# Another written-out order of 679 operations in an S4 convolution and MLP block

## The chip, the cores and the metric

The kernel runs on one core of a Trainium2 chip. The metric is the device time of one execution in microseconds. Five engines work side by side, each through its own queue in program order: TensorE (PE, matrix products; its weight loads are listed as PEld), VectorE (DVE), ScalarE (ACT), GpSimd (POOL) and SyncE (SP). DMA transfers are issued from the queues of SP and POOL.

## What is computed

```python
x = A_u                                   # 1 x 2048 x 512, bf16
h = x + A_ref(layernorm(x))               # S4 convolution
h2 = h + B_ref(layernorm(h))              # MLP
# A_ref: dt = exp(log_dt); K = Re sum_n C_n * exp(dt*A_n*l) * dt*B_n   (128 states n, 2048 lags l)
#        y = irfft(rfft(pad(u)) * rfft(pad(K)))[:2048] + u * Dskip
# B_ref: gelu(y @ w1 + b1) @ w2 + b2      (512 -> 1376 -> 512)
```

## The kernel before

**Two parts.** The front computes the convolution and its residual as 679 recorded operations; the MLP follows as plain code (`mlp`, L1179 and on) and isn't part of the order. The front works on all 2048 rows. Its channels come in two halves of 256 (0 and 1); only the normalisation and the first transform do both at once.

**How the order is set.** Each piece of work is recorded with `S.op` in class `Sched` (L133): the engine, or two allowed engines; what it must follow; which rotating buffer it takes (`acq`) and which it gives back (`rel`). `S.run(ORDER)` (L157 to L178) then emits them in the sequence of the list ORDER (L34). A step of the list is 2 × the operation's number, plus 1 where the second of the two allowed engines is taken; numbers below (#141) are those of operations. Only the relative order on one engine's queue matters for what is issued when; waits between engines follow from the data and the buffers. Two more things follow from the list: a rotating buffer is handed out at the step that takes it (three PSUM buffers "p" of 1024 f32 per partition, through which nearly all TensorE results of the front pass; five "s" for sines, four "a", two "u", two "kf", three "z"), and ScalarE's table set is switched where an operation needs the other set than the one before (L160: natural log and exponential, or sine).

**The stages**, with the lines of their instructions:

- Parameters (`params`, L494 and on): products of A, B, C and dt, exp(dt) (#32), polar form and phase pieces, which are turned by DMA transposes into PL, QL and TL.
- Tables (`tables`): phases by products of one-row operands (L393), sines of them (L126), the scaled half of the table M (L72 on VectorE or L95 on ScalarE; #136 and #141), sums that multiply bases with rows Dp spread by POOL DMAs (L469; L78), the sine of nn (L427, #150), the last rows of M put by SP (L482).
- The block matrix BD for the first transform (#6, L78).
- Normalisation (`norm_in`): sums and squares of six row groups on ScalarE (L876, L878), statistics of the other ten on VectorE (L880), the roots (#209), then 16 times: u (L891 on VectorE or L889 on ScalarE), two products aps (L896), eviction to `a` (L88 ScalarE, L90 VectorE), a DMA to A_dram (L905). When all 16 are written, four DMAs load X back in another layout (L917).
- The kernel of half 0: exponentials (L716), phase products pv and qv (L736, L771), their sines (L126), products Pt and Q (L78), then four groups of 128 small matmuls kps (L801; #334 to #343), evicted as ku, near and far (L805, L120), put to DRAM and read back as kt (L830 to L838).
- The kernel of half 1 in the same way: exponentials by scale (L685, L692, the product with amp at L696), sines, kps (#470, #473, #476, #479), kt (#482 to #488).
- Per half eight times: the spectrum kfps of the kernel (22 matmuls, L991 and L993), evicted to kf; the transform xps of X (8 matmuls, L934 to L937), evicted to X; their product pa (L78); the way back zps (L1026 to L1029), evicted to z, written to Zd (L1070) and turned by a DMA to ZT (L1064; for half 1 #590 to #640).
- Late in the front: W is cleared and filled (L961, L964), the first rows of half 0 (L1084, #659 and #662), and the first four rows of half 1 in four steps (#675 L1119 and L1121, #676 L1126, #677 and #678 L1131), between which stand the last two half ways back (#666, #668).
- The biases of the MLP (#492, L1152 to L1159) on POOL.

Many lines are those of small helpers: L72 and L74 (`ts`), L78 (`tt`), L88 and L90 (`evac`), L95 (`scaled`), L120 (`stt`), L126 (`sines`).

The emitting loop, which the change doesn't touch:

```python
for step in order:
    opts, fn, _, tag, rel = self.ops[step >> 1][:5]
    if tag:
        self.now[tag] = took[step >> 1] = ... room[tag].pop(0)
    fun = self.ops[step >> 1][7]
    if fun not in (None, held):
        held = fun
        self.sets(SETS[fun])
    fn(opts[step & 1][0]) if len(opts) > 1 else fn()
```

Of the kernel before, what the change touches and what calls it, by code (L numbers as in the profile page):

```python
# [31 lines left out]
AT = {"log": 1, "m0": 3, "m1": 3, "bases": 3, "sin0": 3, "exp": (1, 1), "sin": (3, 3)}  # L32
SETS = {1: "natural_log_exp_and_others", 3: "trig_and_small"}
ORDER = [  # L34
# [21 lines left out]
]  # L56


# [1416 lines left out]
```

## Time and profile before

| | |
|---|---|
| median of 3 runs | 271.67 us (270.72 to 272.27) |
| the profiled execution | 271.67 us |
| its span, first to last instruction | 269.9 us |
| PE busy | 235.5 us (87%) |
| DVE busy | 203.8 us (76%) |
| ACT busy | 177.8 us (66%) |
| POOL busy | 44.9 us (17%) |
| table loads on ACT | 7, 9.0 us |

The profile comes from one execution on the chip; all its times run from the start of the span. A row of the timeline gives the start, the duration, the engine, the line, the operation, the tile written and the tiles read, their shape, and in brackets how long the engine had been idle and what ended the idle time. A row of a group gives the busy time of all its instructions, the mean of one in ns, and the idle time ahead of them. A row of windows gives a stretch, its length, then for PE, PEld, DVE, ACT and POOL the busy time and the number of instructions, then the granted clock of TensorE as a share of full speed, the DMA engines' share and GB/s. A row of DMA issues ends with the median time from issue to landing.

### The profile page before, as it was taken

Reading aid. Unit: us, or ns where it says so; the run is one execution under the profiler, and the core shown is the slowest. Engines: PE = TensorE matmul, PEld = TensorE weight load, DVE = VectorE, ACT = ScalarE, POOL = GpSimd, SP = SyncE. Lnnn points to the kernel's source line nnn. Section 1 sums busy time; section 2 is a strip of 40 time slices with the busy share of each in tenths; the row PEclk is TensorE's granted clock in tenths of the full one; section 3 lists DMA queues with packets and bytes.
Section 4 is the critical chain, followed back from the end, with each engine's and each line's share of the span. In section 5 each row is a group of like instructions: output and inputs, shape, how many; then the busy total and the mean of one; then the engine's idle time right before and its main releaser. Section 6 shows DMA issues by size and latency. Waiting matters only on the chain.

```text
span 269.9 us, 6075 instructions
## 1 busy us (share of the span) xinstructions
PE 235.5 (87%) x2369; PEld 152.3 (56%) x2386; DVE 203.8 (76%) x450; ACT 177.8 (66%) x281; POOL 44.9 (17%) x108
## 2 busy tenths in 40 slices
PE   2749966668972999999999999999999999999995
PEld 2413322225740576879988888887864544544443
DVE  3879999999989889999487675889973773772022
ACT  5599999998999988986255255645850730731720
POOL 8752069300001300010033420010000000000000
PEclk9855569999965599999999999999999999999999
DMA  5800266959778559513049499697914014013101
GB/s 137 297 15 1 40 120 137 214 136 179 79 150 256 170 164 350 160 39 87 10 114 251 120 254 261 181 265 217 268 29 107 23 31 105 19 27 94 39 19 58
DMA packets 54968, 35.24 MB, mean 131 GB/s; under 512 B 29050, under 2 KB 53132, under 8 KB 54684
## 3 DMA queue, kind: packets, MB, share of 16 engines
q1 hardware_dynamic: 53036, 30.05, 42.8%
q0 software_dynamic: 1904, 4.81, 7.3%
q8 instruction: 18, 0.29, 0.5%
q14 instruction: 10, 0.08, 0.1%
HBM read 18.65 MB, written 11.21 MB: 111 GB/s over the span
## 4 chain that ended last, share of the span: by engine, by line
PE 64%; DVE 20%; ACT 7%; issue 3%; DMA 3%; SPq 1%; DVEq 0%; ACTq 0%
PE kfps L993 13%; PE o2ps L1279 13%; PE h1ps L1267 13%; PE kps L801 5%; DVE Pt L78 3%; DMA x<-in_A_u_dram 3%; DVE M L78 3%; PE y L1084 2%; DVE a L90 2%; DVE st L880 2%; PE qv L771 2%; PE kfps L991 2%; DVE u L891 2%; PE xps L934 1%; ACT u L876 1%
## 5 line engine op out<-in xcount | busy, mean ns | idle before, releaser
L1269 ACT ACTIVATE hT<-h1ps,b_sb 128x512 bf16<-128x512 f32 (+3 forms) x55 | 32.0, 612 | 36.7 <-PE h1ps L1267 36.7
L993 PE MATMUL kfps<-kt,M 128*128 128x256 bf16 x320 | 40.5, 277 | 0.0
L1267 PE MATMUL h1ps<-y2T,w 128*128 128x512 bf16 (+3 forms) x217 | 39.9, 336 | 0.6 <-DVE y2T L90 0.5
L1279 PE MATMUL o2ps<-w_sb,hT 128*128 128x512 bf16 (+3 forms) x183 | 38.5, 366 | 0.2
L993 PEld LDWEIGHTS <-M 128*128 128x128 bf16 x320 | 31.9, 100 | 4.9 <-issue 0.5
L78 DVE TENSOR_TENSOR ot<-o2ps,h 128x512 bf16<-128x512 f32 (+1 forms) x17 | 11.1, 659 | 30.8 <-PE o2ps L1279 19.0
L1267 PEld LDWEIGHTS <-w 128*128 128x128 bf16 (+1 forms) x220 | 21.9, 100 | 15.2 <-issue 0.6
L1279 PEld LDWEIGHTS <-hT 128*128 128x128 bf16 (+1 forms) x187 | 18.2, 98 | 19.7
L88 ACT CAST kf<-kfps 128x1024 bf16<-128x1024 f32 (+1 forms) x14 | 13.3, 953 | 11.1 <-PE kfps L993 9.3
L126 ACT ACTIVATE sq<-qv 128x1024 bf16<-128x1024 int16 x20 | 19.9, 1049 | 1.1 <-PE qv L771 0.5
L78 DVE TENSOR_TENSOR Pt<-s,Pt 128x1024 bf16<-128x1024 bf16 x32 | 20.2, 687 | 0.0
L801 PEld LDWEIGHTS <-Pt 128*32 128x32 bf16 x1024 | 17.9, 169 | 3.4 <-DVE far L120 1.5
L801 PE MATMUL kps<-Q,Pt 128*32 128x20 bf16 x1024 | 18.7, 221 | 0.6 <-DVE far L120 0.5
L896 PE MATMUL aps<-u,BD 128*128 128x512 bf16 x29 | 10.5, 455 | 10.0 <-DVE u L891 6.7
L78 DVE TENSOR_TENSOR pa<-X,kf 128x1024 bf16<-128x1024 bf16 (+1 forms) x17 | 11.2, 658 | 7.1 <-ACT kf L88 6.7
L126 ACT ACTIVATE s<-pv 128x1024 bf16<-128x1024 int16 x16 | 16.1, 1047 | 0.3 <-DVE Pt L78 0.3
L469 POOL DMA_DIRECT2D Dp<-Dd x24 | 13.4, 566 | 14.6 <-DVE M L78 14.6
L88 ACT CAST z<-zps 128x1024 bf16<-128x1024 f32 x10 | 10.2, 1020 | 7.6 <-PE zps L1029 5.4
L90 DVE CAST a<-aps 128x1024 bf16<-128x1024 f32 x11 | 13.3, 1219 | 0.0
L78 DVE TENSOR_TENSOR Q<-sq,Q 128x1024 bf16<-128x1024 bf16 x20 | 13.2, 688 | 0.0
L771 PE MATMUL qv<-RQ,QL 128*128 128x128 bf16 (+1 forms) x60 | 10.9, 293 | 2.4 <-ACT sq L126 1.1
L78 DVE TENSOR_TENSOR pa<-pa,pb 128x512 bf16<-128x512 bf16 (+1 forms) x34 | 12.4, 407 | 0.6
(245 smaller groups left out, 476.0 us busy)
## 6 DMA issues: line engine op xcount, KB each, us to landing
A_dram<-a SPq DMA_DIRECT2D x16, 256.0 KB, 2.6
X<-A_dram SPq DMA_DIRECT2D x4, 1024.0 KB, 8.2
Zd<-z SPq DMA_DIRECT2D x14, 256.0 KB, 3.2
ZT<-Zd SPq DMA_DIRECT2D x12, 256.0 KB, 3.6
x<-in_A_u_dram SPq DMA_DIRECT2D x4, 512.0 KB, 8.5
out_dram<-ot SPq DMA_DIRECT2D x15, 128.0 KB, 1.7
w_sb<-in_B_w_dram SPq DMA_DIRECT2D x1, 1280.0 KB, 6.8
Dp<-Dd POOLq DMA_DIRECT2D x8, 128.0 KB, 3.5
```

Source lines behind the costliest of these rows:

```text
L78: nc.vector.tensor_tensor(out, a, b, op)
L88: nc.scalar.copy(out, in_)
L90: nc.vector.tensor_copy(out, in_)
L126: nc.scalar.activation(out, v.bitcast(i16)[..., 0:2 * n:2], ACT.Sin, scale=S2PI / 65536)
L469: nc.gpsimd.dma_start(t[o::128 // cnt], bass.AP(row.tensor, row.offset + 1024 * kh, [[0, cnt], [1, 1024]]))
L771: nc.tensor.matmul(v[:, n], lhsT=K.QL[(b + n) // 8][:, (b + n) % 8, :], rhs=K.RQ[:, m0:m1].rearrange("p i c d -> p (i c d)"), start=True, ...
L801: nc.tensor.matmul(kps[32 * g:32 * g + 32, i // 8, at:at + 20], lhsT=Pt[:, :, u, c], rhs=Q[:, :, u, c], start=True, stop=True, tile_positi ...
L896: nc.tensor.matmul(ps[:, h, :], lhsT=K.BD[:, h].rearrange("p a b -> p (a b)"), rhs=cell["u"][:], start=True, stop=True)
L993: nc.tensor.matmul(ps[:, k, c, :], lhsT=K.M[:, t, 2 * k2 + k, c, :], rhs=kt[:, t, :], start=(c == 1 and t == 0), stop=(t == 4))
L1267: nc.tensor.matmul(pt[:fs, 0:n], lhsT=K.w1_sb[:, dc, fc * P:fc * P + fs], rhs=y2T[tb][:, dc, js, :].rearrange("p a b -> p (a b)"), start=( ...
L1269: nc.scalar.activation(hT[tb % 2][:fs, fc, cols], pt[:fs, 0:n], ACT.Gelu_apprx_tanh, bias=K.b1_sb[:fs, fc:fc + 1], scale=1.0)
L1279: nc.tensor.matmul(pt[:], lhsT=h[:fs, fc, jj * P:(jj + 1) * P], rhs=K.w2_sb[:fs, fc, d], start=(fc == 0), stop=(fc == NFC - 1))
```

## The change

Only the list ORDER is another one; it holds the same 679 numbers, a few of them with the other engine. The list is long, so its first, a middle and its last lines stand here:

```diff
 ORDER = [
-    36, 38, 40, 42, 44, 46, 54, 56, 58, 60, 82, 0, 2, 78, 62, 66, 86, 68, 370, 984, 366, 8, 74, 76, 362, 80, 10, 12, 4, 364, 84, 296, 64, 198, 6, 88, 70, 128, 92, 298, 130,
-    132, 374, 378, 376, 72, 380, 94, 274, 372, 382, 134, 384, 136, 160, 90, 164, 138, 368, 392, 284, 48, 140, 124, 142, 390, 96, 166, 388, 278, 144, 126, 146, 396, 168, 148,
...
-    874, 1036, 1038, 862, 924, 876, 864, 726, 1040, 1130, 946, 992, 928, 728, 666, 948, 994, 746, 866, 930, 996, 934, 950, 27, 730, 926, 878, 998, 872, 748, 1046, 25, 936,
...
-    1270, 1272, 773, 1274, 776, 1276, 1286, 1152, 1288, 1085, 1302, 1290, 1306, 1258, 1310, 1318, 1154, 1218, 1324, 1292, 1312, 1278, 1294, 1296, 1320, 1304, 1308, 1314,
-    1326, 1260, 1316, 1330, 1332, 1338, 1341, 1328, 1334, 1350, 1220, 1280, 1344, 1298, 1336, 1352, 1354, 1343, 1346, 1300, 1348, 1356, 1322
+    74, 76, 370, 54, 60, 58, 82, 66, 0, 78, 296, 70, 80, 2, 62, 8, 362, 4, 84, 86, 88, 56, 64, 364, 10, 366, 68, 128, 198, 298, 6, 300, 130, 378, 264, 368, 72, 90, 132, 376,
+    372, 160, 380, 292, 134, 374, 406, 136, 266, 294, 92, 94, 382, 138, 96, 46, 164, 384, 278, 140, 48, 124, 268, 44, 142, 166, 98, 396, 144, 148, 102, 146, 390, 388, 168,
...
+    910, 726, 912, 866, 1036, 944, 714, 874, 728, 860, 926, 920, 914, 946, 876, 746, 878, 716, 948, 950, 742, 990, 1038, 952, 20, 745, 1040, 1126, 954, 748, 958, 992, 956,
...
+    1270, 1218, 772, 777, 1284, 1272, 1274, 1302, 1286, 1180, 1276, 1288, 1324, 1258, 1306, 1318, 1220, 1290, 1292, 1320, 1326, 1278, 1294, 1296, 1241, 1310, 1312, 1200,
+    1304, 1330, 1308, 1261, 1314, 1328, 1280, 1344, 1298, 1316, 1334, 1322, 1350, 1332, 1352, 1338, 1340, 1336, 1343, 1346, 1300, 1348, 1354, 1356
 ]
```

What this does to each engine's queue, by a comparison of the two orders instruction by instruction:

- **ScalarE.** exp(dt) (#32) comes ahead of the sine of BD's factors (#5), the table set changes there once more: eight table loads (L160) for seven. The sine of nn (#150) moves from behind the polar steps to the third place of the queue, ahead of all sums of x. The scale of M (#141) goes to VectorE. Of the u, three (#242, #226, #266) for two (#238, #250) are on ScalarE; of the evictions `a` ahead of the second exponentials it takes five, as before, but others (#216, #228, #244, #268 and #240 for #264, #236, #212, #232 and #240). In half 0's sines the first six are of p, then those of q. In half 1, eleven sines (three p, eight q) stand in a row behind the second exponentials, ahead of the first eviction of a spectrum (#534); before, four stood there.
- **VectorE.** It takes #141 and one u fewer; BD (#6) moves from the third place of the queue to just ahead of spread_p (#55), near the last statistics; two products with amp (#407, #413) stand ahead of the last `a` (#272) where one (#413) stood ahead of the last `a` (#256). It evicts seven spectra kf ahead of the end where it evicted three, and two z instead of four. At the end the first early rows (#660, #663) stand ahead of product #656, the statistics (#661) ahead of the last z (#671).
- **TensorE.** The same operations stand ahead of the first spectrum, which is #513 instead of #503. Ahead of the first kernel product of half 1 (#470) stand, beside what stood there before, spectra #533 and #523, phase products #461, #464, #467 and #431; spectrum #563, phase product #455 and X products #357 and #371 now come behind it. Ahead of the last of the four (#479), spectrum #533 comes in, and X products #365 and #383 and ways back #498 and #568 go behind. At the end #675 stands ahead of #666.
- **POOL.** The biases (#492) go from the start of its queue to behind the clearing of W (#574) and the turn #522. Turns #552, #562, #620 and #630 go by POOL; #512, #502 and #542 go by SP. The put of far for half 0 (#347), the put of near for half 1 (#482) and the kt get #484 go by POOL; the put of far for half 1 (#483) and the kt get #486 by SP. Both residual loads (#579, #580), one load of W1 (#491) and all four fills of W go by SP.
- **SP.** The puts of `a` and the turns come in another sequence; the four X loads still stand behind all 16 puts.

32 rows, old and new, of the table ORDER are left out of this document.

## The prediction

> **What bounds the kernel now.** I read the windows first, cut where the stages change (columns: from:to, length, busy time of each engine with its instructions, granted TensorE clock, DMA share, GB/s).
>
> ```profile
> 20.00:90.00 70.00, 51.50 (x652) 23.74 (x657) 67.63 (x145) 68.52 (x111) 17.54 (x29) 0.77 0.62 128
> 90.00:105.00 15.00, 13.90 (x96) 9.73 (x97) 13.10 (x18) 14.06 (x27) 0.72 (x2) 0.89 0.73 229
> 105.00:183.00 78.00, 77.62 (x1122) 67.97 (x1124) 62.61 (x113) 45.63 (x52) 11.77 (x14) 1.00 0.59 164
> ```
> From 20 to 90 us VectorE (67.63) and ScalarE (68.52) fill the 70 us to 97 and 98%, and TensorE waits for them. From 105 to 183 us TensorE is busy 77.62 of 78 at full clock: 0.38 us is all the air there is. After that the MLP runs, which ORDER doesn't hold. So an order of the same operations can gain in three places: both elementwise engines reach the first spectrum sooner, the 15 − 13.90 = 1.10 us that TensorE idles from 90 to 105 closes, or the last rows come earlier. The chain of waits, second, agrees: TensorE holds 64% of it, VectorE 20%, ScalarE 7%.
>
> ```profile
> PE 64%; DVE 20%; ACT 7%; issue 3%; DMA 3%; SPq 1%; DVEq 0%; ACTq 0%
> ```
> Third, the timeline where one stage passes into the next (start, length, engine, line), and finer windows around it.
>
> ```profile
> 85.27 1.89 PE L896 MATMUL aps<-u,BD 128*128 128x512 bf16 x4 [4.92 <-DVE u L891]
> 90.89 2.34 PE L993 MATMUL kfps<-kt,M 128*128 128x256 bf16 x10
> 91.47 1.22 DVE L90 CAST a<-aps 128x1024 bf16<-128x1024 f32 x1
> 94.52 1.25 PE L993 MATMUL kfps<-kt,M 128*128 128x256 bf16 x10
> 96.50 5.78 SPq L917 DMA_DIRECT2D X<-A_dram  x4
> 102.38 0.28 PE L934 MATMUL xps<-X,M 128*128 128x256 bf16 x1 [0.24 <-ACT kf L88]
> ```
> ```profile
> 80.00:90.00 10.00, 4.29 (x11) 1.08 (x12) 10.00 (x16) 10.00 (x34) 2.42 (x4) 0.50 0.73 201
> 90.00:100.00 10.00, 9.47 (x63) 6.84 (x63) 8.52 (x12) 9.52 (x22) 0.72 (x2) 0.83 0.56 168
> 100.00:110.00 10.00, 9.38 (x76) 6.87 (x76) 9.54 (x16) 8.64 (x10) 0.00 (x0) 1.00 1.08 350
> ```
> TensorE waits 4.92 us for a VectorE `u`, its clock falls to 0.50, and the first half spectrum costs 2.34 instead of 1.25. The last eviction `a` ends at 91.47 + 1.22 = 92.69; the four X loads go out at 96.50 and the first product on X starts at 102.38.
>
> **The change part by part.** The comparison of the two orders shows the same operations, some on the other of their two allowed engines. The profiled execution took 271.67 us, the median of the three too (its span is 269.9, with 1.77 around it), so the sum is made on 271.67.
>
> *ScalarE up to the second set of exponentials.*
>
> ```profile
> L160 ACT ACT_TABLE_LOAD x7 | 9.0, 1283 | 0.9 <-PEq L1459 0.7
> 95.14 1.28 ACT L160 ACT_TABLE_LOAD   x1
> 96.44 2.03 ACT L126 ACTIVATE s<-pv 128x1024 bf16<-128x1024 int16 x2
> L95 ACT ACTIVATE M<-M,cols 128x2048 bf16<-128x2048 bf16 x1 | 2.0, 2019 | 0.0
> L889 ACT ACTIVATE u<-x,mv,r1y 128x512 bf16<-128x512 bf16 x2 | 1.7, 854 | 0.0
> L427 ACT ACTIVATE nn<-nn,pi_t x1: 847/847/847, 27.9 to 27.9; 128x672 f32<-128x672 int32 x1
> L876 ACT ACTIVATE u<-x 128x512 bf16<-128x512 bf16 x6 | 3.8, 631 | 2.3 <-DMA x<-in_A_u_dram 2.2
> ```
> The new order does exp(dt) (#32) ahead of the early sines, so the table set is switched once more: eight loads for seven. A load is 1283 ns and the next sine starts 96.44 − 95.14 = 1.30 later: +1.30. The scale of M (#141, L95) leaves for VectorE: −2.02. A third `u` comes: +0.85. The sine of nn (#150, 0.85) moves from 27.9 us into the 2.2 us in which ScalarE waits for x: −0.85. Sum 1.30 − 2.02 + 0.85 − 0.85 = −0.72, or +0.13 where the wait doesn't take the sine. The Trainium skill, "ScalarE: Activation LUTs", section "What ACT_TABLE_LOAD costs", puts a switch at about 2.66 us, load and a drain of 1.38; by it the sum would be −0.72 + 1.38 = +0.66. The next sine at 96.44 leaves no room for a drain here, so the trace disagrees and 1.30 stays.
>
> *VectorE up to the last `a`.*
>
> ```profile
> 20.00:30.00 10.00, 9.52 (x23) 3.17 (x22) 9.23 (x22) 9.91 (x17) 1.72 (x1) 0.50 0.14 28
> ...
> 40.00:50.00 10.00, 6.32 (x24) 2.06 (x23) 9.55 (x33) 9.97 (x13) 9.69 (x17) 1.00 0.70 135
> 40.92 0.74 DVE L72 TENSOR_SCALAR M<-M,cols 128x2048 bf16<-128x2048 bf16 x1
> L78 DVE TENSOR_TENSOR BD<-wb,mask 128x128 bf16<-128x128 bf16 x2 | 0.7, 604 | 0.0
> L891 DVE TENSOR_SCALAR u<-x,mv,r1y 128x512 bf16<-128x512 bf16 x14 | 5.5, 409 | 0.0
> L696 DVE TENSOR_TENSOR Q<-Q,amp 128x1024 bf16<-128x1024 bf16 x5 | 3.3, 685 | 0.2 <-ACT Q L692 0.2
> ```
> It gains the M scale (0.74, as its twin at 40.92), BD (#6, 0.60), moved out of the idle start to about 39 us, and one more Q product ahead of the last `a` (0.69); it loses one `u` (0.41): +1.62 in all. In the first and the last of these stretches VectorE idles 10 − 9.23 and 10 − 9.55, 1.22 in all; I let 0.9 of the first two fall into it and take +0.7, with ends +0.4 (all of 1.22 taken) and +1.6. So the last `a` ends near 93.4, the X loads go out near 97.2, the first product on X near 103.1. TensorE has the same set of operations ahead of its first spectrum (only another spectrum comes first), and the last `u` stands three evictions ahead of the last `a`: its start (matmuls on M at 90.89) moves by 0 to 0.7, I take +0.2.
>
> *TensorE from 91 to 133.*
>
> ```profile
> L126 ACT ACTIVATE sq<-qv 128x1024 bf16<-128x1024 int16 x20 | 19.9, 1049 | 1.1 <-PE qv L771 0.5
> L90 DVE CAST kf<-kfps 128x1024 bf16<-128x1024 f32 x3 | 3.7, 1222 | 1.3 <-PE kfps L993 1.3
> 103.31 0.59 PE L771 MATMUL qv<-RQ,QL 128*128 128x512 bf16 x2
> 112.90 2.32 PE L801 MATMUL kps<-Q,Pt 128*32 128x20 bf16 x128
> 130.67 2.33 PE L801 MATMUL kps<-Q,Pt 128*32 128x20 bf16 x128
> 147.13 0.27 PE L991 MATMUL kfps<-top,ones 128*128 128x256 bf16 x1
> 147.24 0.60 PE L993 MATMUL kfps<-kt,M 128*128 128x256 bf16 x4
> ```
> ScalarE now does 11 sines in a row (11 × 1.05 = 11.5 us) before its first eviction of a spectrum, formerly four; VectorE evicts the spectra in between (7 instead of 3, 1.22 each). TensorE's results pass through three PSUM buffers, and a buffer comes free about once in 1.05 us for a phase product that takes TensorE 0.59 by itself. Walking the three queues with these durations I get about 3 us idle from 91 to 107, for some 1.1 before. But the new order puts other work there. A matmul of 256 columns follows the one before after 0.11 (147.13 to 147.24): a spectrum of 22 takes 2.4, a phase product (two of 512 columns) 0.44, an X product of 8 takes 0.88. Ahead of the first kernel product (112.90) the new order has one spectrum and three phase products more and two X products fewer: 2.4 + 1.3 − 1.8 = +1.9 of work. I get that product at 115.4: 2.5 later, of which 0.6 is loss. The last of the four, at 130.67 before, I get to end at 132.1 for 133.0, with 1.1 less work done: loss 0.2. I carry +0.3, nearer to the second mark, which holds the whole stretch.
>
> *133 to 183 and the end.* TensorE is full and stays so: 0, at best −0.38.
>
> ```profile
> 177.76 0.27 PE L1026 MATMUL zps<-pa,R 128*128 128x256 bf16 x1
> 178.57 0.27 PE L1119 MATMUL y<-X,ident 128*128 128x256 bf16 x1 [0.22 <-ACT kf L88]
> ```
> The four matmuls at 177.76 (#666) now stand behind the rows that wait for ScalarE at 178.57 (#675): they filled 4 × 0.11 = 0.44 of that wait, which will be 0.22 + 0.44 = 0.66. VectorE has the early rows ahead of the product that #666 needs, which #675's 20 matmuls (2.2 us) cover. I take +0.3 (0 to 0.45).
>
> *Queues, cost nothing.*
>
> ```profile
> L1159 POOL CAST b_sb<-b_bf 128x11 f32<-128x11 bf16 x1 | 3.4, 3382 | 2.9 <-DMA b_bf<-in_B_b_dram 2.9
> ```
> ```profile
> Zd<-z SPq DMA_DIRECT2D x14, 256.0 KB, 3.2
> ...
> ZT<-Zd POOLq DMA_DIRECT2D x4, 256.0 KB, 5.7
> ```
> ```profile
> 171.38 0.37 SPq L1070 DMA_DIRECT2D Zd<-z  x1
> 181.19 1.04 PE L1126 MATMUL y<-ZT,Dm 96*128 96x256 bf16 x8
> ```
> The biases (#492) go from the start to about 152 us on POOL; a load of 2.9 and a cast of 3.38 end before 165, and only the MLP after the last rows reads them. Two late turns of Z (#620, #630) go by POOL. The put ahead of #630 goes out at 171.38 and lands 3.2 later, the turn 5.7 after that, near 180.3; the rows read it at 181.19, now 181.6: 1.3 us of cover. The kernel's put and gets of the second half change queue between 133.0 and the second spectra at 147.13, with 14 us for two transfers. The spreads of Dp no longer wait for a buffer, which only makes them earlier; the residual loads are read behind the last rows.
>
> Sum: 0.3 + 0 + 0.3 = +0.6: **272.3 us**.
>
> **The rivals.** *Starved clock (slower, 274.5).* If the 3 us idle of 91 to 107 lie together, the clock falls as it did after 4.92 us: 80:90 shows 4.29 busy at 0.50. Each half spectrum then costs 2.34 for 1.25; with two of them cold, 2 × 1.1 = 2.2: 272.3 + 2.2. It decides once the granted clock in 97 to 107 is below 1.0. Against it: 40:50 held 1.00 at 6.32 busy, and my idle is cut into pieces under 1 us. For it: 20:30 stood at 0.50 at 9.52 busy, so a busy engine alone doesn't keep the clock. The Trainium skill, "TensorE: Matmul & The Clock Gate", Part 1, lets about 3.4 us of sustained work raise the clock and an idle window as long lower it; by it this rival falls to nothing, but 20:30 differs from the first half of that, and I keep it.
>
> *The front is shorter (faster, 269.9).* ScalarE's −0.72 also frees the sines behind which VectorE waits, and the first spectrum starts 1.5 us sooner (89.2), the 1.10 of idle from 90 to 105 half closes (−0.5) and 133 to 183 gives its −0.38: 271.67 − 2.4 plus 0.6 of my own losses is 269.9. For it: both engines are bound to 98%; against it: VectorE gets more work, not less.
>
> *Late turns (slower, 273.9).* If the eviction of the Z behind #630 comes 2.9 us later than its put at 171.38 shows, the 1.3 us of cover are gone and TensorE waits 1.6 at 181.6: 272.3 + 1.6. For it: ScalarE takes 12 of these evictions for 10, and POOL's way is the slower one; against it: TensorE makes that Z no later than before, two X products for one spectrum standing ahead of it.
>
> *The change isn't what it says.* It moves no operation in or out; nothing to price.
>
> **How the numbers follow.** Forecast 0.42, starved clock 0.22, shorter front 0.20, late turns 0.16. 0.5% of 271.67 is 1.36 us, about what a measurement of this kernel can tell from no change: faster 0.20, same 0.42, slower 0.38. The range goes from the shorter front less 0.4 to the starved clock plus the 0.9 by which VectorE's sum may be dearer: 269.5 to 275.4.
>
> **What would show it.** Eight table loads and none followed by more than 0.1 us; last `a` ending at 93.0 to 94.3; first spectrum at 90.7 to 91.4; TensorE's busy time from 91 to 107 about 13 of 16 at clock 1.00; first kernel product at 114.5 to 116; 105 to 183 over 77 busy; y L1119 behind a wait of about 0.7. It is wrong if the first spectrum starts before 89.5 or after 92.5, or if TensorE idles over 1 us between 133 and 177.

## The result and the profile after

| | before | changed |
|---|---|---|
| median | 272.11 us (270.72 to 273.06, 14 runs) | 273.43 us (271.99 to 274.99, 14 runs) |
| the profiled execution, its span | 271.67, 269.9 | 274.65, 272.6 |
| ratio | | 1.0053 [1.0031, 1.0075] |

The changed kernel is 0.53% slower, 1.4 us on 272.1; forecast was +0.6. The profiled execution has 2.7 us of span over before's. So where the time lies is read from the profile, and how much of it counts from the ratios. Some executions of the runs below were disturbed ones: the times and ratios leave them out, but the profiles of after_again and e_turn are of such, and their marks alone prove nothing.

The windows of the changed kernel, in the stretches of the prediction and around the starved stretch that a rival named:

```profile
20.00:90.00 70.00, 55.50 (x653) 24.08 (x652) 67.42 (x145) 67.16 (x114) 15.71 (x27) 0.67 0.56 123
90.00:105.00 15.00, 13.66 (x106) 9.78 (x104) 14.01 (x20) 13.09 (x24) 0.00 (x0) 0.92 0.67 214
105.00:183.00 78.00, 75.88 (x1098) 65.55 (x1096) 62.66 (x111) 44.83 (x51) 12.42 (x17) 1.00 0.58 162
...
91.00:107.00 16.00, 14.34 (x111) 10.24 (x110) 15.01 (x21) 13.78 (x23) 0.00 (x0) 0.96 0.74 240
97.00:107.00 10.00, 8.38 (x65) 5.53 (x64) 9.76 (x14) 7.94 (x9) 0.00 (x0) 1.00 0.75 246
107.00:133.00 26.00, 26.00 (x653) 22.05 (x651) 23.54 (x42) 16.80 (x20) 0.00 (x0) 1.00 0.30 91
```
VectorE and ScalarE still bound the front (67.42 and 67.16 of 70). TensorE idles 78 − 75.88 = 2.12 us from 105 to 183, where it had 0.38 of air; but from 107 to 133 it is full. Most of the idle time is the two waits at the very end, ahead of L1119 and of L1126, which the next rows show.

The timelines where the stages pass into one another, VectorE's, TensorE's and SP's rows together:

```profile
91.53 1.64 PE L993 MATMUL kfps<-kt,M 128*128 128x256 bf16 x10
92.43 1.22 DVE L90 CAST a<-aps 128x1024 bf16<-128x1024 f32 x1
98.44 5.82 SPq L917 DMA_DIRECT2D X<-A_dram  x4
103.84 0.27 PE L934 MATMUL xps<-X,M 128*128 128x256 bf16 x1
115.43 2.33 PE L801 MATMUL kps<-Q,Pt 128*32 128x20 bf16 x128
130.14 2.32 PE L801 MATMUL kps<-Q,Pt 128*32 128x20 bf16 x128
179.14 0.27 PE L1119 MATMUL y<-X,ident 128*128 128x256 bf16 x1 [0.72 <-ACT kf L88]
181.65 0.27 PE L1029 MATMUL zps<-pa,Rn 128*128 128x256 bf16 x1
183.46 1.03 PE L1126 MATMUL y<-ZT,Dm 96*128 96x256 bf16 x8 [1.55 <-issue]
```
Everything is 0.6 to 2 us later up to the first kernel product, the rows at 179.14 are only 0.57 later than before's 178.57, and then L1126 waits 1.55 us. Those rows read all turned Z of half 1. SP's queue and the chain of waits, ahead of it:

```profile
171.24 0.36 SPq L1070 DMA_DIRECT2D Zd<-z  x1
174.98 0.53 SPq L1064 DMA_DIRECT2D ZT<-Zd  x1
175.60 0.53 SPq L1070 DMA_DIRECT2D Zd<-z  x1
176.18 3.42 SPq L1064 DMA_DIRECT2D ZT<-Zd  x2
```
```profile
171.24 5.62 DMA Zd<-z
176.90 0.46 issue
177.38 4.72 DMA ZT<-Zd
182.09 1.37 issue
183.46 1.03 PE y L1126 x8
```
The put of Z ahead of turn #630 goes out at 171.24, as forecast (171.38), but its turn leaves POOL's queue only at 177.38: 6.14 us later, where 3.2 had been taken. The last turn (#640), the second of the pair that SP issues from 176.18, goes out last, at 176.18 + 3.42 − 0.49 = 179.11. It is most likely what L1126 still waits for after 182.09: there the chain names nothing, but by the view of ZT it is ZT for which L1126 waited 1.5 us. The issues by line show the same for all puts and for SP's turns (KB, then median us to landing; before: 3.2, 3.6, 5.7):

```profile
Zd<-z SPq DMA_DIRECT2D x14, 256.0 KB, 5.2
ZT<-Zd SPq DMA_DIRECT2D x11, 256.0 KB, 6.6
...
ZT<-Zd POOLq DMA_DIRECT2D x5, 256.0 KB, 5.4
```

The first product of the MLP (L1257) ends the stretch, first before, then changed:

```profile
185.74 0.77 PE L1257 MATMUL tps<-ident,y 128*128 128x128 bf16 x8
```
```profile
188.51 0.76 PE L1257 MATMUL tps<-ident,y 128*128 128x128 bf16 x8
```
So of the 2.7 us of span, 0.63 lie ahead of the first spectrum (91.36 for 90.73), −0.06 between it and L1119, 2.20 between L1119 and the first L1257 (9.37 for 7.17), −0.07 behind.

### The profile page after: what moved, and what is told of

Same layout as the page of the kernel before. It is cut to its first block, busy times and chain, and to the rows that moved or that the text cites. A ratio compares the mean times of both kernels' runs of the same rounds, so it can differ in the third digit from the quotient of the medians.

```text
span 272.6 us, 6079 instructions
## 1 busy us (share of the span) xinstructions
PE 242.0 (89%) x2386; PEld 153.4 (56%) x2386; DVE 205.8 (75%) x450; ACT 177.4 (65%) x282; POOL 40.5 (15%) x107
## 4 chain that ended last, share of the span: by engine, by line
PE 56%; DVE 17%; DMA 10%; ACT 6%; SPq 4%; POOL 3%; issue 3%; DVEq 0%; POOLq 0%; ACTq 0%
PE o2ps L1279 13%; PE h1ps L1267 13%; PE kfps L993 9%; PE kps L801 6%; DVE a L90 3%; DMA A_dram<-a 3%; SPq L583 2%; DMA Zd<-z 2%; DVE st L880 2%; DMA X<-A_dram 2%; DMA ZT<-Zd 2%; DVE M L78 2%; PE y L1084 2%; SPq L491 1%; PE aps L896 1%
## 5 line engine op out<-in xcount | busy, mean ns | idle before, releaser
L993 PE MATMUL kfps<-kt,M 128*128 128x256 bf16 x320 | 39.6, 274 | 0.0
L896 PE MATMUL aps<-u,BD 128*128 128x512 bf16 x32 | 13.7, 565 | 5.8 <-DVE u L891 3.8
L88 ACT CAST z<-zps 128x1024 bf16<-128x1024 f32 x12 | 12.2, 1015 | 9.4 <-PE zps L1029 9.0
L88 ACT CAST kf<-kfps 128x1024 bf16<-128x1024 f32 (+1 forms) x10 | 9.3, 933 | 8.6 <-PE kfps L993 8.1
L771 PE MATMUL qv<-RQ,QL 128*128 128x512 bf16 (+1 forms) x64 | 11.6, 298 | 3.8 <-ACT sq L126 2.3
```

The lines of the kernel that those rows point to most:

```text
L88: nc.scalar.copy(out, in_)
L771: nc.tensor.matmul(v[:, n], lhsT=K.QL[(b + n) // 8][:, (b + n) % 8, :], rhs=K.RQ[:, m0:m1].rearrange("p i c d -> p (i c d)"), start=True, ...
L896: nc.tensor.matmul(ps[:, h, :], lhsT=K.BD[:, h].rearrange("p a b -> p (a b)"), rhs=cell["u"][:], start=True, stop=True)
L993: nc.tensor.matmul(ps[:, k, c, :], lhsT=K.M[:, t, 2 * k2 + k, c, :], rhs=kt[:, t, :], start=(c == 1 and t == 0), stop=(t == 4))
```

## The experiments

Theory at the outset: the end makes the loss, and it comes from the DMA traffic. Rivals: the front makes it; or SP's own sequence of puts and turns at the end. All kernels hold the same 679 operations; only ORDER differs. The marks of the profiled executions (us), "load" being the start of the table load that ends the first exponentials, "put to turn" the time from the put of Z ahead of #630 to its turn on POOL:

| kernel | load | load to first kfps | kfps to L1119 | wait at L1126 | put to turn |
|---|---|---|---|---|---|
| before | 48.09 | 42.64 | 87.84 | 0 | |
| changed | 47.35 | 44.01 | 87.78 | 1.55 | 6.14 |
| after_again | 49.00 | 44.84 | 88.32 | 0 | 4.66 |
| h_late | 48.94 | 43.57 | 87.75 | 0 | |
| h_back | 48.05 | 43.43 | 88.08 | 0.44 | 5.64 |
| h_late2 | 48.09 | 43.78 | 88.08 | 0 | 2.95 |
| e_resid | 47.70 | 43.30 | 88.66 | 0.76 | 4.35 |
| e_put | 47.71 | 44.92 | 87.92 | 0.86 | 6.80 |
| e_turn | 47.25 | 43.11 | 88.46 | 3.72 | |
| e_both | 48.63 | 44.22 | 88.45 | 1.56 | 3.01 |
| e_early | 49.17 | 43.47 | 89.58 | 0 | 2.98 |
| e_sput | 47.93 | 43.66 | 91.18 | 0 | 4.74 |
| e_m1 | 49.22 | 43.42 | 88.00 | 0 | 4.28 |
| e_fix | 48.86 | 44.48 | 92.57 | 0 | 3.11 |

**e_resid**, the residual load #580 right behind #579:

```diff
-    1118, 1120, 1159, 760,
+    1118, 1120, 1159, 1161, 760,
...
-    1254, 1256, 1161, 1266,
+    1254, 1256, 1266,
```


> The changed order, with one step moved on SP: the second residual load of X (#580, 512 KB) goes out right behind the first (#579, near 147 us) instead of at 167.05. Theory 1 (this load holds up the puts of Z issued behind it; in the changed kernel those at 168.62 and 171.24 land only about 6 us later, the turns follow late and the rows of L1126 wait 1.55): the two puts land within about 4 us, the wait ahead of L1126 falls below 0.5, the time falls by about 1.2 us against the changed kernel, to a ratio of about 1.001 to before. Theory 2 (the turn #610 standing ahead of the put #639 on SP is what delays the last turn): the wait falls by 0.3 at most, ratio 1.004 to 1.005. Theory 3 (the way of turn #630 by POOL is what is late): no change, ratio 1.005.

Measured 274.73 us, ratio 1.0112 [1.0074, 1.0149]. The wait stays, 0.76, and TensorE waits 0.54 more at 169.61 for a `z` of ScalarE. Moving this one load earlier on the same queue doesn't help.

**e_put**, the turn #610 behind the put #639, so that SP isn't held by a turn whose put hasn't landed:

```diff
-    1258, 1306, 1318, 1220, 1290, 1292, 1320, 1326, 1278, 1294,
+    1258, 1306, 1318, 1290, 1292, 1320, 1326, 1278, 1220, 1294,
```


> The changed order, with turn #610 moved behind put #639 on SP. Theory 2: the put goes out at about 174.6, when its Z is evicted, instead of at 175.60, the last turn lands a microsecond sooner, the wait ahead of L1126 falls to about 0.5 and the ratio to before to about 1.002. Theory 1: the landings stay at 5 to 6 us, the wait falls by 0.4 at most, ratio 1.004. Theory 3: no change, 1.005.

273.10 us, 1.0070 [1.0036, 1.0103]. The put #639 goes out 4.58 us ahead of L1119 for 3.54, and the wait is still 0.86: SP's sequence isn't the cause by itself.

**e_turn**, both late turns on SP:

```diff
-    1241,
+    1240,
...
-    1261,
+    1260,
```


> The changed order, with turns #620 and #630 of Z issued by SP instead of POOL, at the same places of the list. Theory 3 (POOL's turn is the one that is late): the wait ahead of L1126 falls below 0.5, ratio about 1.001. Theories 1 and 2: turn #630 goes out where POOL issued it or later and turn #640 behind it, so the wait stays at 1.5 or grows by up to 1; ratio 1.005 to 1.008.

274.28 us, 1.0109 [1.0058, 1.016]. That POOL takes them isn't what makes the turns late: on SP they cost no less.

**h_late**, the changed order up to #591, the rest in the sequence of before:

> The changed order up to the first spectrum of the second half (147 us), the order of before for everything behind it. Theories 1 to 3, which all put the larger part of the loss behind 147 us: only the 0.57 us by which TensorE is late at 177 us in the changed kernel remain, ratio about 1.002. Rival 4 (the loss comes from the front, the wait at the end only shows it): ratio 1.004 to 1.006.

273.12 us, 1.0052 [1.002, 1.0085], although its profile shows no wait at the end. It seemed to say that what stands ahead of 147 us makes the whole loss; the next runs and the section on the hardware show why it doesn't.

**after_again**, the changed kernel unaltered:

> The changed kernel once more, unaltered, beside the three that follow on the same chip. Theory A (the loss has two parts: VectorE's longer queue up to the last `a` makes TensorE about 1 us late from the X products on, and the end adds 0.44 of lost filler and 0 to 1.7 of waiting for the turns of Z): ratio 1.005 to 1.010, 1.4 to 2.7 us. Rival B (only the end differs): ratio 1.005 or less, and the same as that of the kernel that takes only the end.

273.64 us, 1.0042 [1.0011, 1.0072]. Its profile has no wait at L1126, nor have those of e_m1 and e_sput, whose end is the same: the wait isn't there in every execution of this end.

**h_back** and **h_late2**, the order of before up to #503 (the first spectrum of before) or up to #581, the rest in the sequence of the changed order:

> The order of before up to its first spectrum (about 91 us), the changed order for everything behind it. Theory A: the front's loss goes, what remains is the end, 0.44 and up to 1.7: ratio 1.002 to 1.007, and 0.8 to 1.2 us less than the changed kernel. Rival B: as the changed kernel. Rival C (the row of eleven sines behind 95 us is what costs): as the changed kernel or up to 0.5 us less.

> The order of before up to the first spectrum of the second half (147 us), the changed order behind it: the end alone. Theory A: 0.44 of filler and 0.5 to 1.7 of waiting, ratio 1.003 to 1.008, first product on X at about 102.4 as before. Rival B: the whole loss, the same time as the changed kernel.

h_back: 273.55 us, 1.0052 [1.0033, 1.0072]. h_late2: 272.88 us, 1.0027 [1.0001, 1.0053]. h_back has before's front and loses as much as the changed kernel, so the loss on record lies behind the first spectrum. h_late2 has before's middle too, with the residual loads on POOL where before had them (#491 still goes by SP, near 157), and loses half of it. The two have the same time from first spectrum to L1119, 88.08, and differ at the end. h_back, windows and TensorE:

```profile
160.00:180.00 20.00, 19.28 (x178) 17.11 (x176) 16.31 (x28) 10.90 (x12) 1.96 (x4) 1.00 0.92 254
```
```profile
182.78 1.03 PE L1126 MATMUL y<-ZT,Dm 96*128 96x256 bf16 x8 [0.44 <-issue]
```
h_late2, windows, issues by line from 140 us on, and TensorE:

```profile
160.00:180.00 20.00, 19.28 (x178) 17.09 (x175) 17.11 (x28) 9.99 (x11) 1.85 (x4) 1.00 0.72 208
```
```profile
ZT<-Zd POOLq DMA_DIRECT2D x5, 256.0 KB, 3.6
...
X<-in_A_u_dram POOLq DMA_DIRECT2D x1, 512.0 KB, 5.3
```
```profile
179.95 0.27 PE L1119 MATMUL y<-X,ident 128*128 128x256 bf16 x1 [0.72 <-ACT kf L88]
182.61 1.03 PE L1126 MATMUL y<-ZT,Dm 96*128 96x256 bf16 x8
```
With the loads ahead of 160 us the DMA engines are busy 0.72 instead of 0.92 from 160 to 180, a turn by POOL lands in 3.6 us (h_back: 5.5), put to turn takes 2.95 for 5.64, and L1126 doesn't wait. What its profile still shows is the filler that #666 was: the wait at L1119 is 0.72 here and 0.22 before.

**e_both**, e_resid and e_put together:

> The changed order with both moves on SP: the second residual load (#580) behind the first, and turn #610 behind put #639. In the runs with one of them alone, TensorE still waited 0.76 and 0.86 us ahead of L1126, for 1.55 in the changed kernel. If both delays add up, the wait is under 0.3 us, and the time 0.7 to 1.5 us below the changed kernel on the same chip; if each only uncovers the other way of the turns (POOL's turn #630), the wait stays at 0.7.

274.72 us, 1.0097 [1.0061, 1.0133], the wait 1.56. Put to turn takes 3.01 here, but the last turn, on SP, goes out at 179.55 and lands after 6.10 us. The wait is not bound to one particular transfer.

**e_early**, #579, #580 and #491 back on POOL, the first ahead of #482, the two others behind #487:

```diff
+    998, 962, 1158,
...
+    970, 975, 1160, 982,
...
-    1120, 1159,
...
-    1206, 983,
...
-    1256, 1161,
```


> The changed order with three transfers put back to where they stood before: the two loads of the residual X (#579, #580) and the weight load #491 are issued by POOL again, some 25 to 50 us earlier than SP issues them in the changed order. Theory (a backlog of late loads slows the puts of Z at the end): the transposed loads and puts of 165 to 182 us get shorter, Zd lands in 3 to 4 us instead of 5.2 to 6.3, the wait ahead of L1126 falls from 0.8 to 1.6 us to below 0.2, the stretch from L1119 to the last L1257 from 8.7 to 9.5 us to about 7.7, ratio to before about 1.003. Rival (the wait comes from the order of SP's own issues at the end, whatever was loaded before): the wait stays at 0.4 to 1.6 us, ratio 1.005 to 1.007.

273.91 us, 1.01 [1.0062, 1.0138]. Put to turn falls to 2.98 and the wait is gone, as the theory said. But the ratio isn't 1.003, since a new wait stands in the middle; TensorE and POOL of e_early:

```profile
151.00 1.14 PE L993 MATMUL kfps<-kt,M 128*128 128x256 bf16 x9 [1.32 <-DMA kt<-KD_near]
```
```profile
142.00 0.89 POOL L1176 DMA_DIRECT2D X<-in_A_u_dram  x1
142.69 0.45 SPq L838 DMA_DIRECT2D kt<-KD_far  x1
142.88 0.70 POOL L1150 DMA_DIRECT2D w<-in_B_w_dram  x1
143.24 0.66 SPq L838 DMA_DIRECT2D kt<-KD_near  x1
```
The loads now leave beside the gets of kt for the second spectra, which land behind them and hold TensorE for 1.32 us. At these places the loads trade one wait for another.

**e_sput**, the puts of a (#233, #261) right behind their evictions, two puts of Dg behind the X loads:

```diff
-    868, 34, 830, 852, 466, 989, 522,
+    868, 830, 852, 989,
...
-    840, 32, 1006,
+    840, 1006,
...
+    518, 465, 466,
...
+    660, 521, 522,
...
+    1018, 712, 32, 34,
```


> The changed order with SP's puts of A_dram right behind the evictions that they wait for and the two puts of Dg behind the X loads. Theory (the middle is bounded by TensorE, so an earlier X is worth nothing): X loads leave 0.5 to 1 us earlier, the first X product comes 0.5 to 0.9 us earlier than 12.5 us behind the first kernel product, the stretch from there to L1119 gets longer by as much, and the ratio stays that of the changed kernel, 1.004 to 1.005. Rival (the late X loads are what the changed front costs): the time falls by 0.5 to 0.9 us, ratio 1.001 to 1.002.

276.35 us, 1.018 [1.0149, 1.0212]: both expectations fell, since the edit did the opposite of what it was for. SP and TensorE of e_sput:

```profile
87.81 0.61 SPq L905 DMA_DIRECT2D A_dram<-a  x1
...
91.50 1.47 SPq L482 DMA_DIRECT2D M<-Bd  x2
...
100.35 5.91 SPq L917 DMA_DIRECT2D X<-A_dram  x4
```
```profile
94.19 2.10 PE L993 MATMUL kfps<-kt,M 128*128 128x256 bf16 x9 [2.22 <-DMA M<-Bd]
```
The puts wait for late evictions at the head of SP's queue, the puts of the last rows of M stand behind them and go out at 91.50 (87.49 in the changed kernel), TensorE waits 2.22 us for them, and the X loads leave 6.48 us behind the last `a` instead of 4.79. So an earlier X was not tried. A later one costs what it is late: the first X product comes 15.72 us behind the first spectrum instead of 12.48, and L1119 91.18 instead of 87.78.

**e_m1**, #141 back on ScalarE:

```diff
-    282,
+    283,
```


> The changed order with one of the two M scalings (#141, L72) back on ScalarE, where it stood before. Theory (VectorE bounds the front from 50 to 93 us, so its longer queue costs the changed kernel 0.7 us from the load of the exponentials' table to the first kernel product): that stretch falls from 44.0 by 0.5 to 1 us, while the load itself comes later by what ScalarE spends on the scaling, 0 to 2 us; in sum -0.7 to +1.3 us, ratio 1.002 to 1.009. Rival (the stretch hangs on the clock of TensorE from 48 on, not on VectorE's queue): the stretch stays at 43.5 to 44.5 us and the time rises by all that ScalarE is later.

274.62 us, 1.0124 [1.0095, 1.0153]. Load to first spectrum takes 43.42, 0.6 under the changed kernel's 44.01 (less than the spread of that mark from one execution to the next), and the load itself starts at 49.22, 1.9 later. The loss is the larger, beyond the range that was expected: moving the scale to VectorE was worth 0.7 to 0.8% (1.0124 for 1.0053 and 1.0042, each against before on its own chip).

**e_fix**, e_early and e_sput together with #666 ahead of #675 and its product (#655, #656) ahead of #660:

> The changed order with the three early transfers on POOL, the puts of A_dram as in the run with earlier X, and the end in the order of before (the evictions #655 and #656 ahead of #660 on VectorE, #666 ahead of #675 on TensorE). Theory: the end costs nothing any more (from L1119 to the last L1257 7.2 us, no wait), what is left is 0.7 us from the exponentials' table to the first kernel product: ratio 1.002 to 1.003. Rival (the end was never the loss, since executions without a wait were no faster): the ratio stays at 1.005. Second rival (the front's loss was the late X): ratio below 1.000.

277.54 us, 1.0222 [1.0178, 1.0265]; none of the expectations. It has the bad puts of e_sput and the wait for kt (0.72), its end isn't quite before's (#668 still stands behind #676), and its time says nothing on the rest.

One thing all profiles with the changed end agree on. With the residual loads early (h_late2, e_early, e_fix) the DMA engines are busy 0.61 to 0.72 from 160 to 180, and the puts of Z land in 2.4 to 3.5 us in the median; in the eight others (e_turn, with other turns, aside) they are busy 0.84 to 0.92, and the puts land in 4.1 to 6.4 where the view has a median. But the three changed the loads' time and their queue at once: e_resid and e_both, with both loads by SP near 147, are among the slow ones (6.4 each), so it isn't told apart which of the two counts.

## Why the prediction was right, and where it was too small

The time lies in the range and the sign is the forecast's; the sum was 0.6 for 1.4.

- **ScalarE, −0.72, next sine 1.30 behind a load: right.** The load that ends the first exponentials starts at 47.35 for 48.09, −0.74. The rows of the eighth load:

```profile
94.55 1.28 ACT L160 ACT_TABLE_LOAD   x1
95.85 1.02 ACT L126 ACTIVATE s<-pv 128x1024 bf16<-128x1024 int16 x1
```
  No drain follows the load. But an earlier load is seen only in executions in which TensorE's clock rises early (last section): 47.25 to 47.93 in five profiles, 0.1 to 0.8 earlier, so that the match to 0.02 is luck.
- **VectorE, +0.7 up to the last `a`:** 92.43 + 1.22 = 93.65, +0.96, inside its ends. (The two instructions of BD take 0.7 together, not 0.60; nothing hangs on it.)
- **First spectrum +0.2:** +0.63 in the profile, and over the 11 profiles that have the changed front (e_m1's but for #141) from 90.36 to 93.84, 7 of them past the 92.5 that were to make it wrong. Five of these 7 are the ones with the late clock of the last section. Load to first spectrum takes 42.64, 43.43 and 43.78 with one and the same front of before, 43.11 to 44.92 with the changed one (e_m1 aside): about 0.7 more in the mean, with a spread of 1 to 2. The working took one execution's durations as the kernel's. Where the clock rises early, the earlier load makes up for the longer stretch: the first spectrum starts at 91.39 in the mean of five profiles with the changed front, at 91.36 in that of the three with before's. h_back, with before's front, loses no less than the changed kernel, so in the time none of this is seen either.
- **91 to 133, +0.3: the marks right by luck, the term too large.** The first kernel product starts at 115.43 (115.4), the last ends at 130.14 + 2.32 = 132.46 (132.1). But both count from a first spectrum that is 0.63 late, where 0.2 was taken. From the first spectrum to the first kernel product it is 24.07 us for before's 22.17: 1.90 more, which is the added work of 1.9 and no loss. From 91 to 107 TensorE idles 16 − 14.34 = 1.66 us, not 3. The clock is 1.00 from 97 to 107, the stretch that was to decide: the starved clock didn't come.
- **133 to L1119, 0: right.** 87.78 from first spectrum to L1119 for 87.84.
- **The filler, +0.3:** the wait is 0.72 (0.66 forecast), so the mechanism is right; with 0.72 − 0.22 = 0.50 the whole of it counts and the deduction was wrong. All profiles bear this out: L1119 to the first L1257 takes 7.17 and 7.16 with before's end (before, h_late), 7.66 to 7.77 in the five with the changed end and no wait at L1126 (after_again, h_late2, e_early, e_sput, e_m1), so 0.5 more. h_late2, which has this and not the late loads, loses 0.27% or 0.7 us [0.0, 1.4].
- **Queues, cost nothing: this step failed.** "The residual loads are read behind the last rows" isn't so: VectorE's sums read them (`h<-y,X`, at 176.38), and the rows of L1119 at 179.14. They had landed by then and nobody waited for them. But the loads needn't be late themselves to make the turns late. Issued some 27 us later (146.8 and 167.05 for 119.4 and 140.4), they fall among the last puts and turns. Landing times were taken from before's traffic (3.2 + 5.7), and the cover of 1.3 us was counted on them; they became 6.14 + 4.72, and the wait 1.55. With it the sign "105 to 183 over 77 busy" failed: it is 75.88. The rival of late turns had the place and the price (1.6), but named a late eviction; the put went out on time. h_back less h_late2 gives 0.25%, 0.7 us, for the middle of the order in which those loads stand.

By these two hybrids half of the 0.53% comes from the order behind 147 us, where the filler alone makes 0.5 us, half from the middle, where the late loads stand, and nothing from the front; but the intervals of h_back and h_late2 overlap. That the place of the loads, time and queue together, lengthens the landings is shown by e_early, which moves only them and #491 (puts of Z in 2.4 us for 5.2), and by the other profiles (put to turn 2.95, 2.98 and 3.11 in the three kernels that have them early, 4.28 to 6.80 in all others with this end but e_both). That they make the wait is likely and not shown: it is 0 in those three, but also in three of the eight others with this end. Whether the middle costs its time through this wait stays open too. The four executions of h_late whose clock rises early (last section) have a median of 272.49 for before's 271.71, 0.29%, with the changed middle but before's end, and the one profile of h_late has no wait there; four are too few to decide. The Trainium skill, "DMA: Bandwidth & Descriptors", section "Issuing engines are not separate DMA queues", says that transfers of all issuing engines share the same 16 engines; the traces of h_back and h_late2 fit this: where a residual load of SP's queue falls between 160 and 180, they are busy 0.92 for 0.72, and a POOL turn takes 5.5 us for 3.6.

No version beat before.

## What to carry to other kernels

A landing time read off a profile belongs to the traffic around it: when loads move, even loads nobody waits for, the transfers in their new neighbourhood have to be priced again. A put moved up a queue waits at its head, and all behind it wait too. And a stage whose marks differ by 1 us between executions of one order can't carry a forecast of 0.2: hybrids of the two orders, a dozen executions of each, said more of where the loss lies than single profiles, which misled.

## What was not expected of the hardware

**The clock at the start comes or doesn't.** In the changed order six products of one-row operands (L393) stand ahead of the second group of tps_are, for which VectorE and then ScalarE wait. TensorE and VectorE, in the changed kernel:

```profile
8.97 1.14 PE L514 MATMUL tps_are<-deal,M 128*128 128x128 bf16 x4
10.42 0.38 PE L393 MATMUL v<-gb,si 1*128 1x512 bf16 x1
11.59 0.61 PE L514 MATMUL tps_are<-deal,M 128*128 128x128 bf16 x4
12.24 0.43 DVE L78 TENSOR_TENSOR w<-tps_are,M 128x256 f32<-128x256 f32 x1 [0.74 <-PE tps_are L514]
```
and in h_late, which has the same start, with a row of its windows:

```profile
10.51 0.63 PE L393 MATMUL v<-gb,si 1*128 1x512 bf16 x1
12.78 1.03 PE L514 MATMUL tps_are<-deal,M 128*128 128x128 bf16 x4
13.85 0.42 DVE L78 TENSOR_TENSOR w<-tps_are,M 128x256 f32<-128x256 f32 x1 [2.36 <-PE tps_are L514]
```
```profile
5.00:14.00 9.00, 8.45 (x30) 4.64 (x30) 4.09 (x11) 6.67 (x15) 6.90 (x40) 1.00 0.74 260
```
In h_late every matmul still runs at half speed (0.63 for 0.38) until past 13 us; VectorE waits 1.6 us longer, and the table load comes at 48.94 for 47.35, the same 1.59 later. The windows' granted clock says 1.00 there all the same: the durations show the half speed, the record doesn't. The Trainium skill, "TensorE: Matmul & The Clock Gate", Part 1, has the clock rise after a busy window of about 3.4 us that runs free of the kernel. The changed kernel agrees: TensorE starts at 5.66 and the rise comes between 10.04 and 10.42. h_late goes beyond it, at half speed 7.7 us after its start at 5.07, with one gap of 0.18.

Such executions can be told by their mean clock: 0.949 or more in the five profiles with the late rise (load at 48.63 to 49.17), 0.919 or less in the others. By it, 1 of 88 executions with before's front rose late, and 21 of 91 with the changed front: none of the changed kernel's first 14, 4 of 12 when it ran again, 8 of 12 of h_late, which is why h_late looked as slow as the changed kernel. Of its ten executions in the comparison the six late ones have a median of 273.57, the four others of 272.49. Before's front has both groups of tps_are ahead of such products, and its load comes at 48.05 to 48.09 in three profiles of three. That the place of these products is what makes the rise uncertain was not tested.
